# Packed weights of batches 4 to 7 made for four batches at once, as 64-row tiles, and sorted by batch through DRAM

## The chip, the cores and the metric

The kernel runs on one core of a Trainium2 chip. The time is the device time of one execution in microseconds, as the median of repeated runs. The core's engines work side by side, each in the order of its own queue: TensorE (PE; its weight loads, PEld, are listed apart), VectorE (DVE), ScalarE (ACT), GpSimd (POOL) and SyncE (SP). POOL and SP here mostly start DMAs.

## What is computed

Three stages, in fp32. First an attention in two steps: 32 packed queries `p` per head attend to `k` and `v`, and the result serves `q` as keys and as values.

```python
batch, n_heads, seq, head_dim = (8, 8, 576, 64); n_pack = 32
p_packed = sm_attn(p, k, v)             # softmax(p k^T / 8) v: [8, 8, 32, 64]
out = sm_attn(q, p_packed, p_packed)    # [8, 8, 576, 64]
x = out.transpose(0, 2, 1, 3).reshape(4608, 512)
h = x @ w_in                            # 512 -> 2048
x = (h / (1 + exp(-1.702 * h))) @ w_out # 2048 -> 512
h = max(x @ w1, x @ w2, x @ w3)         # 512 -> 768
return h @ w_out2                       # 768 -> 512
```

## The kernel before

Products are made from split operands: each fp32 value is held as a high and a low part in a reduced format, and `mm3` (line 98) issues three matmuls, low x high, high x low and high x high, into one PSUM bank.

Since the attention's second step ends with a product by `p_packed`, the kernel never forms `x`. It multiplies `p_packed` into `w_in` first. The result, `pw`, has 8 x 32 = 256 rows for a batch instead of 512, and the first feed-forward layer is a product of the softmax weights `at` with `pw`. Heads come in two groups g of four; a chunk c (0 to 3) of `w_in` is 128 rows, two heads; n (0 to 3) is a quarter of 512 columns of the 2048.

The first feed-forward part (FF1) runs as 256 units. Unit n takes one batch, one half of 288 tokens (hf) and one chunk fc of 128 columns: `h_unit` is 6 matmuls, two groups by `mm3`, from `at` and `pw`; tanh on ScalarE, a product on VectorE; `g_unit` splits the result, `out_unit` is 12 matmuls into four accumulating banks `acc`, two units later. Batches 0 and 1 are units 0 to 63 in alternating pieces; from batch 2 on a batch takes 32 units, so batch 4 starts at unit 128, and its quarter n is first used by unit 128 + 4n.

`pw` of batches 0 and 1 is made by `pw1_unit`. For batches 2 to 7 two batches share a matmul: `sps[pr, g]` holds `p_packed` of the batches 2 pr and 2 pr + 1 with zeros where head and batch don't belong together, so that `pw_unit(pr, c, n)` (line 383) takes 128 rows of `w_in` and gives 128 rows of result, two heads by two batches by 32. There are 16 calls for each of the three pairs. Its bank is a `pa` tile; `evac` (line 127) casts it to the high part on ScalarE and subtracts on VectorE, once for each half of the partitions, straight into the two batches' `pw` tiles. `load_wi` (line 378) fetches the split `w_in` chunk from DRAM (`wsc`) on POOL's queue, into a tile of tag `x`, of which there are four; the FF1 output `x2` uses the same tag.

The attention of a batch and group is a `Group` with steps: `load_pk`, `split_pk`, `load_v`, `s1` (scores, into two `pa` banks), `sm1`, `t1` and `t1r` (transposes), `load_q`, `pv`, `pt` (line 296: transposes the result and puts its split into `sps`, and an unsplit copy into `ptf` for the second step), `s2`, `sm2`, `sm3`, `tr2`. `s1`, `pv` and `s2` write 64 columns each, in two tiles of the array. The pool `ps_a` has two banks, which s1, t1, t1r, pv, pt, s2 and the `pw` units share.

`main` (line 804) writes the order by hand. Every step is put in a list with a due time, `add(t, fn, ...)`, and the list is sorted; a step's instructions are issued in that order, and where a tile isn't free, another ready step may come first. `tn[n]` is the due time of unit n, 2.55 apart from unit 11 on, a planned time and no measured one. `attention(t, b, g, stretch, dq)` puts the steps of a group from t on, and delays `load_q`, `s2` and what follows by dq. For the pairs 2 and 3 (batches 4 to 7) the four groups start 20 apart from `tn[64]` and `tn[128]`, and the 16 `pw_unit` calls lie within the last 32 units ahead of the pair's first use (`R_`, line 39). After the last attention step (`last_at`, line 897) the conversion of the second layer's weights starts (`Piece`), 8.5 apart.

Of the kernel before, what the change touches and what calls it, by code (L numbers as in the profile page):

```python
# [8 lines left out]
F32 = mybir.dt.float32  # L9
F32R = mybir.dt.float32r  # L10
# [6 lines left out]
B, H, S, D, NP = 8, 8, 576, 64, 32  # L17
DM, DFF, DFF2 = 512, 2048, 768
NT = B * S
P = 128  # L20
TB = 512
# [7 lines left out]
KD = DM // P  # L29
NQ = DFF // TB  # L30
# [7 lines left out]
Q_ = [12, 9, 9, 8]  # L38
R_ = [32, 23, 17, 5]
# [4 lines left out]
def tile_packed_attention_moe(  # L44
# [13 lines left out]
    nc = tc.nc  # L58
# [5 lines left out]
    def stage_pool(name, bufs, side):  # L64
        return tc.alloc_tile_pool(name=name, bufs=bufs, side=side, reuse_waits="tile")
# [3 lines left out]
    spp = stage_pool("spp", 1, "right")  # L69
    ap_ = stage_pool("ap", 1, "right")  # L70
# [5 lines left out]
    dram = ctx.enter_context(tc.tile_pool(name="dram", bufs=1, space=bass.MemoryType.DRAM))  # L76

    def f(t):
        return t.bitcast(F32)
# [5 lines left out]
    def w_tile(name, dt=F32R):  # L85
        return wp.tile([P, 2, 2, TB], dt, tag="w", name=name)

    def u_tile(name, dt=F32):
        return up.tile([P, S], dt, tag="u", name=name)

    def x_tile(name, dt=F32):
        return up.tile([P, 4 * HALF], dt, tag="x", bufs=4, name=name)

    def pa_tile(name):
        return ps_a.tile([P, TB], F32, tag="pa", name=name)
# [21 lines left out]
    wsc = dram.tile([2, NQ, 2, P, 2, TB], F32R, name="wsc")  # L117

    wsa = dram.tile([9, P, 2, 2, 3, P], F32R, name="wsa")
    wss = dram.tile([9, P, 2, 2, 4, P], F32R, name="wss")  # L120


# [4 lines left out]
    def evac(o, hi, lo):  # L127
        nc.scalar.copy(hi, o)  # L128
        nc.vector.tensor_tensor(out=lo, in0=o, in1=f(hi), op=ALU.subtract)  # L129
# [69 lines left out]

    at = {}  # L200
    sps = {}
    ptt = {}

    class Group:
# [27 lines left out]

        def load_q(self):
            self.q = self.load_t(q, "q")


        def s1(self, hf):
# [58 lines left out]
        def pt(self):  # L296
            o = pa_tile(f"ptp_{self.n}")
            self.mm = nc.tensor.transpose(o[:, :P], self.pn, ident)
            o3 = o[:, :P].rearrange("p (c n) -> p c n", c=2)
            self.ptf = ap_.tile([P, 2, D], F32, tag="ptf", bufs=2, name=f"ptf_{self.n}")  # L300
            if self.b < 2:
                t = u_tile(f"pt_{self.n}", F32R)
                nc.gpsimd.memset(f(t).rearrange("p (x n) -> p x n", x=2)[:, :, D:D + P], 0.0)
                to = ptt[self.b, self.g] = [t[:, HALF * x:HALF * x + 2 * P] for x in range(2)]
            else:
                key = self.b // 2, self.g
                if key not in sps:
                    sps[key] = [
                        spp.tile([P, 2 * P], F32R, tag=f"sp{self.g}{x}", name=f"sp{x}_{key[0]}_{key[1]}")
                        for x in range(2)  # L310
                    ]
                to = sps[key]
            hi, lo = (
                t[:, D:D + P].rearrange("p (c n) -> p c n", c=2) if self.swap
                else t.rearrange("p (c n) -> p c n", c=4)[:, 0:4:3] for t in to
            )
            nc.scalar.copy(self.ptf, o3)
            evac(o3, hi, lo)
# [56 lines left out]
    wi = {}  # L375
    pw = {}
# [6 lines left out]
    def pw_unit(pr, c, n):  # L383
# [8 lines left out]
        for x in range(2):  # L392
            r = slice(D * x, D * x + D)
            t = pw[2 * pr + (x ^ c & 1), n][:, g]
            evac(o[r], t[r, 0], t[r, 1])


    def pw1_unit(b, g, n):
        if g == 0:
            pw[b, n] = w_tile(f"pw_{b}_{n}")  # L400
        o = pa_tile(f"pw_{b}_{g}_{n}")
        for c in range(2):
            t = ptt[b, g]
            w = wi[0, 2 * g + (c ^ b & 1), n]
            mm3(o, [x[:, c * P:c * P + P] for x in t], (w[:, 0], w[:, 1]), c == 0, c == 1)
        hi, lo = (pw[b, n][:, g, x] for x in range(2))
        if n < 1 and b == 0:
            nc.scalar.copy(hi, o)
            nc.tensor.matmul(o, nident, hi, start=False, stop=True, skip_group_check=True)
            nc.scalar.copy(lo, o)  # L410
        else:
            evac(o, hi, lo)
# [33 lines left out]
    start = {}  # L446
# [315 lines left out]
    def add(t, fn, *a):  # L762
        plan.append((t, len(plan), fn, a))
# [28 lines left out]
    tpt, tend = {}, [0.0]  # L792

    def attention(t, b, g, stretch, dq=0.0):
        ts = []
        for k, (dt, fn) in enumerate(Group(b, g).steps()):
            after = {9: 7, 13: 12, 12: 11, 11: 10, 10: 8, 8: 6, 6: 5, 5: 3, 3: 1, 4: 2, 1: 0}.get(k)
            tk = t + dt * stretch + (D_[k] if b == 0 else 0) + (dq if k in (7, 9, 11, 12, 13) else 0)
            ts.append(tk if after is None else max(tk, ts[after] + .05))
            add(ts[-1], fn)  # L800
        tpt[b, g] = ts[10] + .05
        tend[0] = max(tend[0], ts[-1])

    def main():
# [10 lines left out]
        tn = [0.0] * 300  # L815
        t = T0
# [31 lines left out]
        for n in range(NQ):  # L848
            def tc_(kk):
                base = 7 + 6.49 * kk if n == 0 else tn[start[0, n]] - 22 + 7 * (kk - 4 * n)  # L850
                return base + K_[kk]
            for g in range(2):
                t = tc_(kk)
# [8 lines left out]
                kk += 1  # L862


        for pr in range(1, B // 2):
            b0 = 64 * (pr - 1)
            for idx, (b, g) in enumerate([(0, 0), (1, 0), (0, 1), (1, 1)]):
                if pr == 1:
                    attention(tn[0] + 70 + 18 * idx, 2 * pr + b, g, 1.2, 0 * b)
                else:  # L870
                    attention(tn[b0] + 20 * idx + 2, 2 * pr + b, g, 1.2, 38 * b)
            for n in range(NQ):
                for c in range(KD):
                    qn = Q_[n] if pr == 1 else R_[n]
                    qs = 1 if pr == 1 else 3
                    nn = start[2 * pr, n] - max(1, int(qn) - int(c * qs))
                    tp = max(tpt[2 * pr, c // 2], tpt[2 * pr + 1, c // 2])
                    add(max(tn[nn - 7] + .3, tp - 8), load_wi, pr, c, n)
                    add(max(tn[nn] + .3, tp), pw_unit, pr, c, n)


        def open_late():
# [17 lines left out]
        for idx in range(18):  # L900
            pc = Piece(idx // 2, idx % 2)
            t = TP + idx * TP_[1] if idx < 14 else TB0 - 10 + (idx - 14) * 10.5
# [5 lines left out]
        for fc in range(NF2):  # L908
            t = max(TP + 14 * TP_[1] + TP_[2] * fc, tn[225])
# [11 lines left out]
        for n in range(9 * NBLK):  # L921
            j, r = divmod(n, 9)
# [24 lines left out]
    if True:  # L947
        main()
        for _, _, fn, a in sorted(plan, key=lambda s: s[:2]):
            fn(*a)  # L950
        late["f"].release()
        late["x"].release()
        spp.release()
# [53 lines left out]
```

## Time and profile before

| | |
|---|---|
| median of 3 runs | 1333.19 us (1333.18 to 1334.12) |
| the profiled execution | 1333.64 us, of which span 1331.5 us |
| TensorE busy | 1308.8 us, 98% of the span, 8614 matmuls |
| VectorE, ScalarE, GpSimd busy | 69%, 40%, 8% |
| FF1 and attention | to 783 us of the span |
| second feed-forward layer | 783 us to the end |

The rows below come from that one execution. A row of the timeline gives the start in us from the span's start, the duration in us, the engine, the line, the operation, output <- input tiles, shapes and how many like it follow one another. A matmul's listed duration overlaps the next one's: what it costs the engine is the step from its start to the next start. In brackets stand the idle time ahead of an instruction and what ended it.

### The profile page before, as it was taken

How to read it: one execution, taken by the hardware profiler on the slowest of the kernel's cores; microseconds unless marked ns; L12 is line 12 of the kernel's file. 1: busy time of each engine (PE TensorE's matmuls, PEld its weight loads, DVE VectorE, ACT ScalarE, POOL GpSimd, SP SyncE). 2: the span in 40 equal slices, each digit the busy share in tenths (PEclk: the TensorE clock that was granted, in tenths of full speed). 3: DMA queues.
4: the chain of work that ended last, by engine and by line, in shares of the span. 5: the costliest groups of instructions: out<-in, count | busy, mean ns of one | idle time of the engine just before them, and what ended most of it. 6: DMA issues, size and time to landing. Idle time of an engine off the chain costs nothing.

```text
span 1331.5 us, 22347 instructions
## 1 busy us (share of the span) xinstructions
PE 1308.8 (98%) x8614; PEld 1229.7 (92%) x8614; DVE 919.9 (69%) x1896; ACT 533.3 (40%) x1140; POOL 107.4 (8%) x218
## 2 busy tenths in 40 slices
PE   6899999999999999999999999999999999999998
PEld 5699898989999989999999999999899899999997
DVE  6899976874756565669999889736556467366461
ACT  3466544554445444446656442311311313123111
POOL 1200001100000000000000001001011011010000
PEclk9899999999999999999999999999999999999999
DMA  9697734643323331236655649847657476575451
GB/s 338 211 403 300 251 107 139 193 123 120 106 80 100 103 102 54 82 112 195 207 200 191 206 160 360 294 169 252 223 188 264 151 261 239 172 254 197 174 174 48
DMA packets 88875, 249.70 MB, mean 188 GB/s; under 512 B 10177, under 2 KB 39361, under 8 KB 81857
## 3 DMA queue, kind: packets, MB, share of 16 engines
q0 software_dynamic: 24640, 132.66, 29.2%
q1 hardware_dynamic: 64128, 115.62, 25.4%
q8 instruction: 68, 1.11, 0.3%
q14 instruction: 39, 0.31, 0.1%
HBM read 204.47 MB, written 43.78 MB: 186 GB/s over the span
## 4 chain that ended last, share of the span: by engine, by line
PE 92%; DVE 4%; DMA 2%; issue 1%; ACT 1%; SPq 0%; POOL 0%; ACTq 0%; DVEq 0%; POOLq 0%
PE acc L100 10%; PE p L101 10%; PE p L100 10%; PE p L102 10%; PE acc L102 10%; PE acc L101 9%; PE h L100 5%; PE h L102 5%; PE h L101 5%; PE accb L101 4%; PE accb L102 4%; PE accb L100 4%; PE pw L100 1%; PE pw L101 1%; PE pw L102 1%; PE pv L287 1%
## 5 line engine op out<-in xcount | busy, mean ns | idle before, releaser
L100 PE MATMUL acc<-g,wo 128*128 128x288 f32 x1024 | 303.6, 299 | 0.0
L102 PE MATMUL acc<-g,wo 128*128 128x288 f32 x1024 | 300.6, 294 | 0.0
L101 PE MATMUL acc<-g,wo 128*128 128x288 f32 x1024 | 299.6, 293 | 0.4 <-POOL g L468 0.3
L100 PEld LDWEIGHTS acc<-g,wo 128*128 128x128 f32 x1024 | 191.4, 188 | 10.5 <-issue 5.3
L101 PEld LDWEIGHTS acc<-g,wo 128*128 128x128 f32 x1024 | 192.2, 188 | 4.3 <-issue 1.0
L102 PEld LDWEIGHTS acc<-g,wo 128*128 128x128 f32 x1024 | 192.0, 188 | 1.6 <-issue 1.5
L460 ACT ACTIVATE t<-h 128x288 f32<-128x288 f32 x256 | 104.8, 410 | 181.7 <-PE h L102 179.8
L461 DVE SCALAR_TENSOR_TENSOR t<-t,h 128x288 f32<-128x288 f32 x256 | 114.7, 450 | 84.7 <-ACT t L460 83.3
L100 PE MATMUL h<-at,pw 128*128 128x288 f32 x512 | 155.2, 304 | 1.3 <-DVE t L461 1.1
L101 PE MATMUL h<-at,pw 128*128 128x288 f32 x512 | 151.7, 296 | 0.3 <-POOL at L125 0.3
L102 PE MATMUL h<-at,pw 128*128 128x288 f32 x512 | 151.3, 296 | 0.0
L466 ACT CAST g<-t 128x288 fp32r<-128x288 f32 x256 | 110.6, 433 | 93.6 <-DVE t L461 92.4
L468 DVE TENSOR_TENSOR g<-t,g 128x288 fp32r<-128x288 f32 x254 | 114.9, 453 | 34.7 <-ACT g L466 33.8
L681 DVE TENSOR_TENSOR u<-s,p 128x384 f32<-128x384 f32 x54 | 29.9, 553 | 119.1 <-PE p L102 119.1
L101 PE MATMUL p<-x_T,ws 128*128 128x384 f32 x324 | 108.2, 334 | 0.0
L100 PE MATMUL p<-x_T,ws 128*128 128x384 f32 x324 | 108.2, 334 | 0.0
L102 PE MATMUL p<-x_T,ws 128*128 128x384 f32 x324 | 108.1, 334 | 0.0
L100 PEld LDWEIGHTS h<-at,pw 128*128 128x128 f32 x512 | 96.3, 188 | 9.7 <-issue 5.6
L101 PEld LDWEIGHTS h<-at,pw 128*128 128x128 f32 x512 | 96.4, 188 | 1.7 <-POOL at L125 1.3
L102 PEld LDWEIGHTS h<-at,pw 128*128 128x128 f32 x512 | 96.4, 188 | 0.1
L711 ACT COPY s<-p 128x384 f32<-128x384 f32 x54 | 25.9, 479 | 161.8 <-PE p L102 161.7
L129 DVE TENSOR_TENSOR pw<-pw,pw 64x512 fp32r<-64x512 f32 (+1 forms) x110 | 74.9, 686 | 18.2 <-ACT pw L128 17.2
(175 smaller groups left out, 2637.1 us busy)
## 6 DMA issues: line engine op xcount, KB each, us to landing
ws<-wss POOLq DMA_DIRECT2D x54, 1024.0 KB, 7.6
wa<-wsa POOLq DMA_DIRECT2D x54, 768.0 KB, 4.6
wi<-wsc POOLq DMA_DIRECT2D x48, 512.0 KB, 3.9
k<-in_k SPq DMA_DIRECT2D x16, 576.0 KB, 4.2
q<-in_q SPq DMA_DIRECT2D x16, 576.0 KB, 3.9
x2d<-x SPq DMA_DIRECT2D x16, 576.0 KB, 4.0
wss<-ws SPq DMA_DIRECT2D x36, 256.0 KB, 4.0
xr<-x2d SPq DMA_DIRECT2D x24, 384.0 KB, 4.1
```

The source lines that it names most:

```text
L100: nc.tensor.matmul(o, al, bh, start=start, stop=False, skip_group_check=more)
L101: nc.tensor.matmul(o, ah, bl, start=False, stop=False, skip_group_check=more)
L102: nc.tensor.matmul(o, ah, bh, start=False, stop=stop, skip_group_check=more)
L129: nc.vector.tensor_tensor(out=lo, in0=o, in1=f(hi), op=ALU.subtract)
L287: self.mm = nc.tensor.matmul(o[x * D:x * D + D, :P], self.et[:, c * P + x * D:c * P + x * D + D], self.v[:, c, y * P:y * P + P], start=c = ...
L460: nc.scalar.activation(t, o, AF.Tanh, scale=0.5 * 1.702)
L461: nc.vector.scalar_tensor_tensor(out=t, in0=t, scalar=1.0, in1=o, op0=ALU.add, op1=ALU.mult)
L466: latest["act"] = nc.scalar.copy(g[:, 0], gt[n])
L468: latest["dve"] = eng.tensor_tensor(out=g[:, 1], in0=gt[n], in1=f(g[:, 0]), op=ALU.subtract)
L681: latest["dve"] = nc.vector.tensor_tensor(out=o, in0=a, in1=b, op=op)
L711: latest["act"] = nc.scalar.copy(self.s1, self.b1)
```

## The change

For the batches 4 to 7 `p_packed` is no longer put into `sps`. `pt` copies it, unsplit, to a DRAM tile `ptd` (8 pieces), and `load_q` reads it back for `s2`. `split_q` reads it a second time and puts the split into `sq[g]`, whose columns are ordered by chunk, then by the four batches: 4 x 32 = 128 columns, each with one head's 64 rows in the upper or the lower half of the partitions. No zeros are kept. `pwq_unit(c, n)` then multiplies each half, 64 rows, by the same half of the `w_in` chunk: two heads, each three matmuls of 512 columns on 64 rows of the array, in turns, into two `pa` banks. Each bank holds one head for four batches. Both are evacuated whole into tiles of tag `x` and stored to a DRAM tile `pwd` on SP's queue; `load_pw(b, n)` reads the batch's rows back with four DMAs on POOL's queue.

There are 16 calls of `pwq_unit` for 32 of `pw_unit`. The order changes with it: the first halves of the attention of all four batches (to `pt`) start from `tn[64]` on, the groups of batches 4 and 5 15 apart, those of 6 and 7 between them; the second halves of 6 and 7 stay after `tn[128]`, by a larger dq. `split_q` is due from `tn[92]`, the 16 `pwq_unit` from `tn[95]`, 6.9 apart (the last between units 135 and 136), `load_pw` 6 units ahead of the first use for batch 4 and 14 for the others. `last_at` moves from 496.15 to 482.15 of planned time.

```diff
+    ptd = dram.tile([8, P, 2, D], F32, name="ptd")
+    pwd = dram.tile([NQ, KD, 2, P, 2, TB], F32R, name="pwd")
...
         def load_q(self):
             self.q = self.load_t(q, "q")
+            if self.b >= 4:
+                self.ptf = ap_.tile([P, 2, D], F32, tag="ptf", bufs=2, name=f"ptq_{self.n}")
+                nc.sync.dma_start(self.ptf, ptd[2 * (self.b - 4) + self.g])
...
+            elif self.b >= 4:
+                nc.scalar.copy(self.ptf, o3)
+                nc.sync.dma_start(ptd[2 * (self.b - 4) + self.g], self.ptf)
+                return
...
+    def split_q(b, g):
+        if g not in sq:
+            sq[g] = [spp.tile([P, 2 * P], F32R, tag=f"sp{g}{x}", name=f"sq{x}_{g}") for x in range(2)]
+        t = ap_.tile([P, 2, D], F32, tag="ptf", bufs=2, name=f"ptr_{b}_{g}")
+        nc.sync.dma_start(t, ptd[2 * (b - 4) + g])
+        k = (b & 1) * 2 + (b - 4) // 2
+        for x in range(2):
+            r = slice(D * x, D * x + D)
+            hi, lo = (y.rearrange("p (c m) -> p c m", c=2)[r, :, k * NP:k * NP + NP] for y in sq[g])
+            evac(t[r, :, x * NP:x * NP + NP], hi, lo)
+
+    def pwq_unit(c, n):
+        g = c // 2
+        cs = slice(c % 2 * P, c % 2 * P + P)
+        w = wi.pop((2, c, n))
+        o = [pa_tile(f"pwq_{c}_{n}_{x}") for x in range(2)]
+        for k, (y, z) in enumerate(((1, 0), (0, 1), (0, 0))):
+            for x in range(2):
+                r = slice(D * x, D * x + D)
+                nc.tensor.matmul(o[x], sq[g][y][r, cs], w[r, z], start=k == 0, stop=k == 2)
+        for x in range(2):
+            t = x_tile(f"pws_{c}_{n}_{x}", F32R)[:, :2 * TB].rearrange("p (a b) -> p a b", a=2)
+            evac(o[x], t[:, 0], t[:, 1])
+            nc.sync.dma_start(f(pwd[n, c, x]), f(t))
+
+    def load_pw(b, n):
+        pw[b, n] = w_tile(f"pw_{b}_{n}")
+        k = (b & 1) * 2 + (b - 4) // 2
+        for y in range(2):
+            for x in range(2):
+                r = y * D + x * NP
+                nc.gpsimd.dma_start(
+                    pw[b, n][r:r + NP],
+                    pwd[n, (y ^ b & 1)::2, x, k * NP:k * NP + NP].rearrange("g p a b -> p g a b"),
+                )
...
+        for idx, (b, g) in enumerate(order):
+            attention(tn[64] + 15 * idx - 10, 4 + b, g, 1.2, 30 + 10 * b)
+        for idx, (b, g) in enumerate(order):
+            attention(tn[64] - 3 + 15 * idx, 6 + b, g, 1.2, tn[128] - tn[64] + 20 + 8 * idx)
...
+        tq = [max(tn[92], *(tpt[b, g] for b in range(4, B))) + 3 * g for g in range(2)]
+        for b in range(4, B):
+            for g in range(2):
+                add(tq[g], split_q, b, g)
+        for n in range(NQ):
+            for c in range(KD):
+                t = max(tn[95] + 6.9 * (4 * n + c), tq[c // 2] + 2)
+                add(t - 12, load_wi, 2, c, n)
+                add(t, pwq_unit, c, n)
+            for b in range(4, B):
+                add(max(t + 3, tn[start[b, n] - 6 - (8 if b > 4 else 0)]), load_pw, b, n)
```

## Rows read from the trace of the kernel before

**Rows 1.** The page: busy us and share by engine; chain that ended last.

```profile
PE 1308.8 (98%) x8614; PEld 1229.7 (92%) x8614; DVE 919.9 (69%) x1896; ACT 533.3 (40%) x1140; POOL 107.4 (8%) x218
...
PE 92%; DVE 4%; DMA 2%; issue 1%; ACT 1%; SPq 0%; POOL 0%; ACTq 0%; DVEq 0%; POOLq 0%
```

**Rows 2.** Stage table: stretch, its us, engines' busy us, clock, DMA share, GB/s.

```profile
209.00:292.00 83.00, 82.14 (x588) 74.03 (x585) 63.22 (x136) 44.70 (x101) 8.99 (x19) 1.00 0.54 164
...
450.00:540.00 90.00, 89.85 (x692) 81.13 (x691) 51.36 (x121) 40.17 (x104) 3.16 (x8) 1.00 0.25 80
...
610.00:660.00 50.00, 48.82 (x350) 47.17 (x349) 49.56 (x119) 31.63 (x69) 1.58 (x3) 1.00 0.65 212
```

**Rows 3.** Timeline of TensorE: the first matmul of two neighbouring FF1 units.

```profile
402.38 0.29 PE L100 MATMUL h<-at,pw 128*128 128x288 f32 x1
...
404.75 0.29 PE L100 MATMUL h<-at,pw 128*128 128x288 f32 x1
```

**Rows 4.** Groups of instructions by shape: count, busy us, mean ns, idle ahead.

```profile
L129 DVE TENSOR_TENSOR pw<-pw,pw 64x512 fp32r<-64x512 f32 x96 | 65.7, 687 | 17.3 <-ACT pw L128 16.5
...
L380 POOL DMA_DIRECT2D wi<-wsc x48 | 25.5, 532 | 287.2 <-PE pw L102 240.7 <-DVE a L337 9.8 <-DVE ws L576 9.7
...
L100 PE MATMUL pw<-wi,sp 128*128 128x512 f32 x48 | 19.3, 403 | 1.0 <-DMA wi<-wsc 0.9
```

**Rows 5.** Timeline of TensorE: a `pw` unit's first matmul, and what follows the unit.

```profile
442.30 0.40 PE L100 MATMUL pw<-wi,sp 128*128 128x512 f32 x1
...
443.01 0.29 PE L100 MATMUL acc<-g,wo 128*128 128x288 f32 x1
```

**Rows 6.** Timeline of TensorE around `s1` (L242), read in narrow windows.

```profile
450.01 0.29 PE L102 MATMUL h<-at,pw 128*128 128x288 f32 x1
450.23 0.46 PE L242 MATMUL s<-k,pbd 128*64 128x288 f32 x2
...
450.23 0.14 PEld L242 LDWEIGHTS s<-k,pbd 128*64 128x64 f32 x2 [0.16 <-issue]
...
450.53 0.41 PE L242 MATMUL s<-k,pbd 128*64 128x288 f32 x2
...
450.77 0.41 PE L242 MATMUL s<-k,pbd 128*64 128x288 f32 x2
...
451.36 0.40 PE L100 MATMUL acc<-g,wo 128*128 128x288 f32 x1
451.59 0.30 PE L101 MATMUL acc<-g,wo 128*128 128x288 f32 x1
```

**Rows 7.** Timeline of TensorE: the largest hole after 610 us.

```profile
626.63 0.40 PE L100 MATMUL h<-at,pw 128*128 128x288 f32 x1 [0.88 <-DVE t L461]
```

**Rows 8.** Timeline of VectorE: the second subtract of the unit of rows 5.

```profile
445.15 0.69 DVE L129 TENSOR_TENSOR pw<-pw,pw 64x512 fp32r<-64x512 f32 x1 [0.28 <-ACT pw L128]
```

**Rows 9.** DMA issues from 209 to 782 us: count, KB each, us to landing.

```profile
x2d<-x SPq DMA_DIRECT2D x14, 576.0 KB, 4.0
...
wsa<-wa SPq DMA_DIRECT2D x32, 192.0 KB, 2.0
...
wraw<-in_w SPq DMA_DIRECT2D x36, 128.0 KB, 3.7
...
xr<-x2d SPq DMA_DIRECT2D x4, 384.0 KB, 6.8
...
v<-in_vr SPq DMA_DIRECT2D x7, 64.0 KB, 3.3
```

**Rows 10.** Timeline: an `s1` and the second exponential that reads it.

```profile
317.01 1.19 PE L242 MATMUL s<-k,pbd 128*64 128x288 f32 x8
...
319.88 0.49 ACT L259 ACTIVATE e<-s,st 128x288 f32<-128x288 f32 x1
```

**Rows 11.** Timeline of TensorE: an `s1` in two parts.

```profile
267.63 0.71 PE L242 MATMUL s<-k,pbd 128*64 128x288 f32 x4
268.27 0.40 PE L100 MATMUL acc<-g,wo 128*128 128x288 f32 x1
```

More of the change, by code (lines that the diff above doesn't have):

```diff
@@ L201, in tile_packed_attention_moe @@
     sps = {}
+    sq = {}
     ptt = {}
@@ L862, in main @@
                 kk += 1
[L865 to L879, printed above, removed]
+        order = [(0, 0), (1, 0), (0, 1), (1, 1)]
+        for idx, (b, g) in enumerate(order):
+            attention(tn[0] + 70 + 18 * idx, 2 + b, g, 1.2)
+        for idx, (b, g) in enumerate(order):
+            attention(tn[64] + 15 * idx - 10, 4 + b, g, 1.2, 30 + 10 * b)
+        for idx, (b, g) in enumerate(order):
+            attention(tn[64] - 3 + 15 * idx, 6 + b, g, 1.2, tn[128] - tn[64] + 20 + 8 * idx)
+        for n in range(NQ):
+            for c in range(KD):
+                nn = start[2, n] - max(1, int(Q_[n]) - c)
+                tp = max(tpt[2, c // 2], tpt[3, c // 2])
+                add(max(tn[nn - 7] + .3, tp - 8), load_wi, 1, c, n)
+                add(max(tn[nn] + .3, tp), pw_unit, 1, c, n)
+        tq = [max(tn[92], *(tpt[b, g] for b in range(4, B))) + 3 * g for g in range(2)]
+        for b in range(4, B):
+            for g in range(2):
+                add(tq[g], split_q, b, g)
+        for n in range(NQ):
+            for c in range(KD):
+                t = max(tn[95] + 6.9 * (4 * n + c), tq[c // 2] + 2)
[3 more added lines that the diff above has]
+                add(max(t + 3, tn[start[b, n] - 6 - (8 if b > 4 else 0)]), load_pw, b, n)
         def open_late():
```

## The prediction, made before the changed kernel was run

> **What bounds the kernel now.** I read the page's busy shares and its chain of waits first. TensorE is busy 98% of the span and carries 92% of the chain [rows 1], so the time is TensorE's instruction stream with almost no holes. A cut in VectorE, ScalarE or DMA work pays only where one of them made TensorE wait. The stage table comes next [rows 2]: from 450 to 540 us VectorE is busy 51 of 90 us and TensorE 89.85. Only from 610 to 660 us is VectorE full, 49.56 of 50, and there TensorE has 1.2 us of holes. Last, the timeline of one FF1 unit: a unit (6 h matmuls, 12 acc matmuls) repeats every 404.75 - 402.38 = 2.37 us [rows 3], 0.132 us a matmul. This step from start to start is what an instruction costs; the durations of 0.29 and 0.40 us overlap.
>
> **What is removed.** The packed weights of batches 4 to 7 take 32 of the 48 calls of `pw_unit` [rows 4]; each is three 512-column matmuls, 443.01 - 442.30 = 0.71 us [rows 5], a step of 0.235. 32 x 0.71 = 22.7 us of TensorE, all on the path. With them go 64 casts, 64 subtracts of 0.69 us [rows 4] and 16 of the `wi` loads.
>
> **What is added on TensorE.** 16 calls of `pwq_unit`, each three pairs of matmuls; each pair has the two heads on 64 rows of the array each, into two banks. No row of before shows 64-row tiles. The nearest are the 64-column tiles of `s1` [rows 6]: the two weight loads start together, so do the two matmuls, and the pairs start at 450.23, 450.53 and 450.77, 0.24 us apart. That is no proof of overlap: 0.12 us a matmul is about the 0.132 of a full 288-column one. Loads starting together are what two tiles working side by side would give, and I take a pair at 0.235, the step of one 512-column matmul; one after the other it is 0.47. Less than 0.235 I exclude: every tile still streams 512 columns.
> The same rows price entering and leaving a tile shape. In: 450.01 to 450.23 is 0.22 instead of 0.132 (+0.09). The first pair takes 0.30 instead of 0.24 with 64-column weights; I double the excess for 128 columns, +0.11. Out: the fourth pair (450.77 + 0.24 = 451.01) to 451.36 is 0.35 instead of 0.24 (+0.10); then 451.36 to 451.59 is 0.23 instead of 0.132 (+0.10). Together 0.40 us. A unit is 3 x 0.235 + 0.40 = 1.11 us, 16 are 17.7 us. Net: 22.7 - 17.7 = **-5.0 us**; without the switch -11.4, without overlap 16 x (6 x 0.235 + 0.40) = 29.0, that is +6.3.
> The trace, then, leaves the overlap open, and my reading rests on the loads that start together. The Trainium skill, "TensorE: Matmul & The Clock Gate", section "Measured speedup vs the span model", gives 3.07 times for four 32-row tiles; scaled from that, as an estimate, a pair would be 0.235 x 4 / 3.07 = 0.31 us and the net -1.4 us instead of -5.0.
>
> **Evacuations.** A unit of before takes two casts and two subtracts on half the partitions; a unit of after takes as many on all 128, for twice the work. So VectorE and ScalarE lose half of these: 32 x 0.69 = 22 us of VectorE over the whole, and none is left from 610 to 660 us, where six units lay (12 subtracts, 8 us). There TensorE waited 0.88 us for the VectorE step of an h unit [rows 7]. The weight conversion (`Piece`) of the second feed-forward layer starts 14 us of plan earlier (`last_at` 496 to 482) and spreads into the room. I take **-1.0 us** (0 to -1.2, the holes of the window; a loss I exclude, since VectorE only loses work).
>
> **The trip through DRAM.** `pwq_unit(3, 3)` is due between units 135 and 136; its result is first used by unit 140 (batch 4, fc 12). On TensorE lie between: 1.11 + 4 x 2.37 = 10.6 us. The chain: matmuls 1.1; evacuation about 2.5 (in before 445.15 + 0.69 - 443.01 = 2.8 [rows 5, 8], where the second cast waited for the first subtract); the SP store 4.0; about 0.5 for the POOL issue behind the other half's; the load 3.7 [rows 9]. Sum 11.8, so TensorE waits **+1.2 us**, once. With the fastest store of the rows (2.0) and 2.2 for the evacuation it is 9.5 and no wait; with 6.8 us for both transfers 18.2, a wait of 7.6. Behind TensorE's wait nothing else can run but two acc units. The other 15 units have 5 or more units of room. POOL's 64 issues of 0.53 us [rows 4] less 16 are 25 us on an engine that is 8% busy [rows 1]: hidden. SP waits for each subtract before it issues a store; what queues behind (later q, k and v loads, x2d stores) is due units later.
> `split_q` reads eight 64 KB pieces back through the two buffers of tag `ptf`, which `load_q` of (5, 0) and (4, 1) also hold until their `s2`. At 3.3 us a load [rows 9] and about 1 us of splitting, the first four end some 12 us after `s2` of (5, 0); on TensorE `pwq_unit(0, 0)` comes 126.0 - 112.8 = 13 us after it (due times, with 2.37 us a unit and the steps above). No margin to speak of: **+0.5 us** (0 to 2).
>
> **The denser first half of attention.** Eight groups run s1 to pt between units 62 and 88 where four were, beside ten `pw_unit` calls of batches 2 and 3. `s1` holds both banks of `ps_a`, 317.01 to 319.88 and a cast time later [rows 10], 2.9 to 3.4 us. In the due order three or four of the eight meet a bank that is not free. Before, such a meeting did not stop TensorE: `s1` was cut in two with acc matmuls between [rows 11], at the price of one more switch: 268.27 - 267.63 = 0.64 for two pairs, less 2 x 0.24, and the slow first matmul, 0.3 us in all. Three cuts: **+1.0 us** (0 to 7.7, below). VectorE has room: 63 of 83 us were busy there [rows 2], and four more first halves are some 7 us.
>
> **Sum.** -5.0 - 1.0 + 1.2 + 0.5 + 1.0 = -3.3 us. The profiled execution took 1333.64 us (span 1331.5 and 2.1 us around it), which gives 1330.3; it lies 0.45 us above the median of 1333.19, so for the median **1329.9 us**. Two of the terms are waits that fall on single points, so the forecast's own range, all at their mild ends or most at the hard ones, is 1326.5 to 1334.
>
> **Rivals.**
> *Weights not loaded ahead.* Tiles overlap, but a pair's weights wait for the pair before. Each of the 32 later pairs then pays the 0.10 us of a 128-column load seen after the switch [rows 6]: +3.2, 1333.1 us. For it: no row shows 64-row tiles. Against it: in `s1` the later pairs follow at 0.24, with no load time between.
> By the skill's scaled pair of 0.31 us the time would be 1329.9 + 48 x 0.075 = 1333.5, the same outcome.
> *The change doesn't do what it says:* the heads run one after the other. +11.3, 1341.2 us, slower. For it: 0.12 us a matmul in [rows 6] is what a serial pair would also show. Against it: the loads start together.
> *Slower by the banks.* In units 63 to 82 TensorE waits instead of running other units. The waits, from the 2.9 and 3.4 us hold and the 2.8 us evacuation of a `pw_unit`: `pw` after `s1` of (4,0) 0.8, s1(6,0) behind a `pw` 2.2, s1(5,0) 0.6, pv(6,0) 1.6, s1(7,0) 2.2, s1(5,1) 0.3: 7.7 us instead of 1.0, 1336.6 us. It decides once about six of the 7.7 us stand as holes. Against it: [rows 11] and 82.14 of 83 us busy there [rows 2].
> *Slower by the store and reload.* 7.6 us at unit 140 instead of 1.2: 1336.3 us. For it: the 6.8 us loads in the same stretch [rows 9]; against it: DMA is idle most of 373 to 450 us by the other rows' 3.7 to 4.0.
> *No price for the switch* with 64-row tiles: -6.4, 1323.5 us.
>
> The Trainium skill, "TensorEngine Tiling (Array Packing)", section "Restrictions and Gotchas", has a rule against the change: row tiles must write different banks, which raises the pressure on PSUM. Here that is the third rival, at 1336.6 us. From unit 108 on no other user of the two banks is due beside `pwq_unit`, which no run here shows yet.
>
> **How the numbers follow.** Forecast 0.57, weights not ahead 0.14, serial 0.12, banks 0.08, reload 0.05, no switch price 0.04. 0.2% (2.7 us, what a measurement of this kernel can tell from no change) puts the lines at 1330.5 and 1335.9. Of the forecast's 0.57, 0.46 lies below 1330.5 and 0.11 between. Faster 0.46 + 0.04 = 0.50; same 0.11 + 0.14 = 0.25; slower 0.12 + 0.08 + 0.05 = 0.25. The range 1326.5 to 1337 holds the forecast, the second rival and both bank and reload cases, 0.84, and leaves out serial and no switch price, 0.16.
>
> **What would show it.** The two matmuls of a `pwq` pair start within 0.02 us and the pairs 0.24 us apart (serial: each 0.24); a unit takes 1.1 us of TensorE. VectorE falls by some 20 us, and the hole near 625 us is gone. At unit 140 TensorE waits about 1 us for a load of `pw`; s1 appears cut in two three more times between 200 and 300 us. Wrong if pairs step by over 0.3 us, if TensorE's holes between units 62 and 95 sum to over 3 us, or if `pwq` units are themselves cut in two, since then their halves can't overlap.

## The result, and the profile after

The changed kernel takes 1344.57 us (median of 5 runs, 1341.5 to 1345.54) against 1334.12 us for the kernel before (1333.18 to 1334.76): a ratio of 1.0076, interval 1.0065 to 1.0088. It is 0.8% slower, where 1329.9 us and "faster" were forecast. The profiled execution took 1345.24 us, its span 1343.4.

The page: busy us by engine, and the chain that ended last (compare [rows 1]).

```profile
PE 1311.5 (98%) x8614; PEld 1224.5 (91%) x8614; DVE 898.5 (67%) x1872; ACT 520.2 (39%) x1116; POOL 133.7 (10%) x266
...
PE 85%; DVE 7%; DMA 4%; ACT 2%; issue 2%; SPq 0%; POOL 0%; DVEq 0%; ACTq 0%
```

VectorE lost 21.4 us of work, as forecast. But the chain, which was 92% TensorE, is now 85%, and VectorE and DMA took the difference: TensorE waits. Where, the stage table tells (columns as in [rows 2]):

```profile
209.00:292.00 83.00, 82.25 (x585) 70.72 (x583) 60.34 (x138) 45.44 (x106) 9.73 (x22) 1.00 0.59 184
450.00:540.00 90.00, 89.46 (x655) 83.75 (x655) 48.54 (x102) 37.65 (x87) 19.22 (x36) 1.00 0.85 211
610.00:660.00 50.00, 45.48 (x328) 44.67 (x327) 42.47 (x107) 25.54 (x57) 1.34 (x3) 0.97 0.63 198
```

The first two stretches are nearly as busy as before (82.14 and 89.85 us). From 610 to 660 us TensorE lost 3.3 us against [rows 2], and VectorE, which was full there, is now idle 7.5 of 50 us. Of TensorE's waits after 600 us, this is the whole list (engine, line, what was waited for: us, times, longest):

```profile
PE h L100 <- DVE t L507: 7.2, 2, 3.9
PE acc L101 <- DVE g L514: 0.7, 2, 0.4
PE acc L100 <- DVE x L540: 0.4, 2, 0.2
```

That is 8.3 us, against 1.1 us in the kernel before, nearly all in two stops (timeline of TensorE, in brackets the idle time ahead of the instruction):

```profile
619.71 0.40 PE L100 MATMUL h<-at,pw 128*128 128x288 f32 x1 [3.91 <-DVE t L507]
...
714.25 0.61 PE L100 MATMUL h<-at,pw 128*128 128x288 f32 x1 [3.25 <-DVE t L507]
```

Behind both stands VectorE, which waits for a DMA (timeline of VectorE):

```profile
613.50 0.46 DVE L514 TENSOR_TENSOR g<-t,g 128x288 fp32r<-128x288 f32 x1 [0.16 <-ACT g L512]
618.59 0.69 DVE L574 SCALAR_TENSOR_TENSOR wa<-c,wraw 128x512 fp32r<-128x512 f32 x1 [4.64 <-DMA wsa<-wa]
619.20 0.45 DVE L507 SCALAR_TENSOR_TENSOR t<-t,h 128x288 f32<-128x288 f32 x1
...
713.07 0.43 DVE L565 TENSOR_SCALAR c_o<-wraw_o 128x512 int32<-128x512 int32 x1 [3.66 <-DMA wraw_o<-in_w_out]
```

VectorE runs in order. At 613.96 us it reaches a step of the weight conversion that needs a store (`wsa`, started at 612.01 us) to have landed, and waits 4.64 us; the `t` step of an FF1 unit is queued behind it (619.20) and TensorE's next h unit behind that (619.71). And this is what POOL had started shortly ahead of both stops, batch 7's reloads of packed weights, four transfers each (timeline of POOL):

```profile
609.22 2.12 POOL L439 DMA_DIRECT2D pw<-pwd  x4 [7.34 <-PE h L102]
...
702.82 2.10 POOL L439 DMA_DIRECT2D pw<-pwd  x4 [17.32 <-PE h L102]
```

The other two of batch 7's bursts, at 599.73 and 683.38 us, have no stop over 0.4 us behind them.

The DMA issues from 606 to 618 us say what that does to the transfers beside them (count, KB each, median us to landing):

```profile
pw<-pwd POOLq DMA_DIRECT2D x4, 256.0 KB, 6.5
wss<-ws SPq DMA_DIRECT2D x2, 256.0 KB, 3.8
wsa<-wa SPq DMA_DIRECT2D x1, 192.0 KB, 6.5
```

The `wsa` store took 6.5 us, where the same store took 2.0 us in [rows 9]. The Trainium skill, "DMA: Bandwidth & Descriptors", section "Issuing engines are not separate DMA queues", says that transfers started by different engines run on the same 16 DMA engines and interleave. The trace agrees in that the two were under way together: SP's store from 612.0 to 618.5 us, POOL's four loads started from 609.2 us on and landed from 613.7 to 618.2 us.

The stops cost a second time. The clock after them (window, us, busy us of the five engines, then the granted clock, DMA share, GB/s):

```profile
616.00:620.00 4.00, 0.29 (x2) 0.30 (x3) 1.41 (x3) 0.32 (x1) 0.00 (x0) 1.00 0.28 60
620.00:624.00 4.00, 4.00 (x22) 3.99 (x21) 2.82 (x10) 1.81 (x5) 0.00 (x0) 0.63 0.73 250
624.00:628.00 4.00, 4.00 (x31) 4.00 (x30) 3.75 (x9) 2.62 (x6) 0.00 (x0) 0.94 0.29 112
...
706.00:710.00 4.00, 4.00 (x32) 4.00 (x32) 3.41 (x10) 2.29 (x5) 0.00 (x0) 1.00 1.15 307
710.00:714.00 4.00, 0.99 (x8) 0.77 (x6) 0.93 (x3) 0.47 (x1) 0.00 (x0) 0.90 1.09 325
714.00:718.00 4.00, 3.75 (x15) 3.75 (x16) 4.00 (x10) 2.53 (x7) 0.00 (x0) 0.50 0.20 77
718.00:722.00 4.00, 4.00 (x25) 4.00 (x25) 3.79 (x9) 2.33 (x5) 0.00 (x0) 0.75 0.42 131
```

TensorE stood still, and behind each stop it ran for a while at the lower clock, 0.50 (1.2 of 2.4 GHz): 15 matmuls from 714 to 718 us, where there were 32 from 706 to 710 us. Summed over the five windows from 620 us on that are below 1.00, 4 us times what is missing, that is 1.5 + 0.2 + 0.4 + 2.0 + 1.0 = 5.1 us. Counted by units it comes out alike: from FF1 unit 180 to unit 228 the changed kernel falls 13.1 us behind the one without the reload (e1 below), 8.1 us of it are waits, and 5.0 are left.

**The account.** The sum of the prediction gave 1330.3 us for the profiled execution; it took 1345.24, 14.9 us more. Waits after 600 us: 8.3, where 0.1 was left in the sum (1.1 less the 1.0 that was booked as gain): +8.2. Half clock behind the two stops: +5.1. From 40 to 52 us the granted clock was 0.72 instead of 0.86: 12 x 0.14 = +1.7, which is this execution's and not the change's: FF1 unit 4 starts 1.8 us later than in the kernel before, and in e1 and e2 below, whose programs are the same up to 200 us, 0.2 us later and 0.2 us earlier. The waits between 372 and 512 us (1.1 and 0.5 us) came to what was booked for the trip through DRAM and `split_q` (1.7). That makes 15.0. That it closes to 0.1 us is in part luck: the waits that were measured there are others than the ones that were booked.

### The profile page after: what moved, and what is told of

It is laid out like the page before. It is cut to its first block, busy times and chain, and to the rows that moved or that the text cites. A ratio compares the mean times of both kernels' runs of the same rounds, so it can differ in the third digit from the quotient of the medians.

```text
span 1343.4 us, 22585 instructions
## 1 busy us (share of the span) xinstructions
PE 1311.5 (98%) x8614; PEld 1224.5 (91%) x8614; DVE 898.5 (67%) x1872; ACT 520.2 (39%) x1116; POOL 133.7 (10%) x266
## 3 DMA queue, kind: packets, MB, share of 16 engines
q8 instruction: 68, 1.11, 0.4%
## 4 chain that ended last, share of the span: by engine, by line
PE 85%; DVE 7%; DMA 4%; ACT 2%; issue 2%; SPq 0%; POOL 0%; DVEq 0%; ACTq 0%
PE p L101 10%; PE p L102 10%; PE p L100 10%; PE acc L100 8%; PE acc L101 8%; PE acc L102 8%; PE h L100 4%; PE h L102 4%; PE h L101 4%; PE accb L102 4%; PE accb L101 4%; PE accb L100 4%; PE pv L293 1%; DMA wsa<-wa 1%; PE s L335 1%
## 5 line engine op out<-in xcount | busy, mean ns | idle before, releaser
L102 PE MATMUL accb<-wo,g 128*128 128x512 f32 x216 | 84.1, 390 | 0.0
```

What stands on the lines that cost most here:

```text
L102: nc.tensor.matmul(o, ah, bh, start=False, stop=stop, skip_group_check=more)
```

## Experiments

The theory from these rows (T1): the reloads of batch 7 crowd the loads and stores of the weight pieces. The first rival (T2): the pieces, which start 14 us earlier, do it alone.

**e1: no reload for batch 7.**

```diff
+        if b == 7:
+            nc.gpsimd.memset(f(pw[b, n]), 0.0)
+            return
```

> The changed kernel with batch 7's four reloads of packed weights left out (the tiles are filled with zeros by POOL, so batch 7's first feed-forward layer has wrong weights; all TensorE, VectorE and ScalarE instructions stay). Theory T1 (the reload bursts of batch 7 crowd the second layer's weight pieces): the holes of 4.1 and 3.4 us and the half clock behind them (about 4.7 us) go; 1344.6 - 7.5 - 4.7 = 1332 to 1334 us. Rival T2 (the pieces' earlier start alone makes the holes): both holes stay, 1343 to 1345 us.

1331.71 us, ratio 0.9981 (0.9972 to 0.9991). T1 holds: 13 us are gone with 4 MB of transfers; beside them only the four fills on POOL are new. T2 falls: the pieces start as early as in the changed kernel and the stops are gone. After 600 us one wait of 0.2 us is left (TensorE's waits):

```profile
PE acc L100 <- DVE x L543: 0.2, 1, 0.2
```

This is also what the rest of the change is worth: -2.5 us by the ratio, -2.3 by the medians.

**e2: pieces at their old due times.** `last_at = max(...) + 14.0`.

> The changed kernel with the weight pieces of the second feed-forward layer due 14 us later, where they lay before the change; the reloads are as in the changed kernel. T1: the reloads still meet pieces, perhaps other ones, so at least one hole of 3 us or more with half clock behind it stays, 1338 to 1345 us. T2: the holes go, 1332 to 1334 us.

1354.08 us, ratio 1.0147 (1.0122 to 1.0171). The later start doesn't help: stops remain (2.1 us of an h unit's wait for VectorE at 629 us), and now the pieces are also done too late, so that the second layer begins with a wait of 6.7 us for VectorE.

**e5: the reloads in four parts on SP.**

```diff
+            for q in range(4):
+                add(tn[(183, 191, 211, 221)[n] + 2 * q], load_pwq, 7, n, q, nc.sync)
```

> The changed kernel with each of batch 7's four reloads cut into its four transfers, started two units (about 5 us) apart on SP's queue instead of all at once on POOL's. The bytes are the same. T1: no burst, the holes go or fall below 1 us each, 1332 to 1336 us. T2: unchanged, 1343 to 1345 us. If it is the total of bytes and not the burst: smaller holes on more places, 1337 to 1343 us.

1334.85 us, ratio 1.0011 (1.0001 to 1.0020). 9.7 us of the 13 are back with the same bytes. The rest of its waits after 600 us is 3.6 us; the longest, 1.7 us, has VectorE busy and not waiting.

**e6: reloads to 128 rows.** The four batches' rows alternate in DRAM, so a reload is one transfer of 1 MB to 128 partitions or two of 512 KB to 64.

> The changed kernel with the rows of the four batches interleaved in DRAM, so that a reload is one transfer to 128 partitions (even batches) or two to 64 (odd ones) instead of four to 32; same bytes. If the narrow shape makes the burst (T4): 4 KB pieces at about 174 ns instead of 360, the burst half as long, holes 0 to 2 us each, 1332 to 1338 us. If the bytes alone do it (T1 without T4): holes unchanged, 1342 to 1345 us.

1352.02 us, ratio 1.0128 (1.0111 to 1.0145): worse. The wider shape doesn't shorten the burst. Its 512 KB loads after 600 us took 7.2 us to landing, the 256 KB loads of the changed kernel 6.3; TensorE waited 7.8 us for VectorE's `t` step instead of 7.2. The rows also lie apart in DRAM now, which this run doesn't separate from the shape. TensorE waited 4.1 us more at 475 us; that place is taken up below.

**e9, e10, e11: burst, queue or place.** e9 starts the four parts on SP at one due time instead of two units apart. e10 and e11 leave them on POOL and make each wait for an FF1 unit, by a copy of four elements from that unit's g tile into the rows that the load then overwrites:

```diff
+            nc.gpsimd.tensor_copy(out=pw[b, n][r:r + NP, 0, 0, :4], in_=gt[u][r:r + NP, 1, :4])
```

> The spread kernel with the four transfers of a reload started back to back again, still on SP's queue. T1 (the burst is what hurts, whichever queue starts it): holes of 2 to 4 us come back, 1338 to 1346 us. Rival (POOL's queue was the cause, not the burst): as the spread kernel, 1333 to 1336 us.

1336.23 us, ratio 1.0021 (1.0010 to 1.0031). It doesn't separate anything: SP's instruction order put other transfers between the parts again (starts at 609.9, 612.2, 618.1 and 620.7 us, in e5 609.1, 611.3, 617.3 and 619.8).

> The changed kernel with batch 7's reloads held to their due units on POOL's own queue: each of the four transfers of a reload first lets POOL copy four elements of the g tile of unit 210, 212, 214, 216 (then 218 and on) into its rows, so that transfers start 2 units, about 5 us, apart instead of four at once as soon as a buffer is free. Same bytes, same queue, same four-batch units. T1 (four transfers at once crowd the pieces): no hole over 2 us, 1332 to 1336 us. Rival (POOL's queue itself is slow, however the transfers are spread): holes as in the changed kernel, 1340 to 1345 us.

1338.96 us, ratio 1.0038 (1.0025 to 1.0050).

> As the paced kernel, but the four transfers of a reload start together again, at units 210, 218, 226 and 234. If four at once is what hurts: each burst leaves a hole of 2 to 4 us where it meets a piece, 1338 to 1346 us. If it was only the place of the first two bursts (600 and 609 us, at the first pieces): 1332 to 1336 us.

1337.97 us, ratio 1.0029 (1.0017 to 1.0040). On POOL's queue, held to units 210 to 240, four at once and four spread cost the same, so "four at once" is not the cause. e10 fits neither of its ranges; e11 lies at the edge of T1's, with 4.1 us of `h` waits, the longest 2.6. e10 has few waits up to 700 us, and then one of 3.5 us of TensorE for ScalarE, which waits for VectorE, which waits for a load (timeline of VectorE):

```profile
732.74 0.43 DVE L572 TENSOR_SCALAR c<-wraw 128x512 int32<-128x512 int32 x1 [3.71 <-DMA wraw<-in_w]
```

What the kernels with the reload share is that it costs: 3.1 us (e5), 4.5 (e9), 6.3 (e11), 7.2 (e10) and 12.9 (as changed) above the kernel without it. Bursts on POOL's queue cost 12.9 us where POOL took them, as soon as buffers were free, and 6.3 us at units 210 to 234, so the place counts. Whether SP's queue (e5, e9) is the better one by itself isn't shown, since there the place differs too.

**e4, e12: the same bursts in the kernel before.** Each adds four times four 256 KB transfers from DRAM to DRAM that nobody reads.

> The kernel before with nothing of the change, but with four extra bursts on POOL's queue, each of four 256 KB transfers from DRAM to DRAM that nobody reads, due at units 182, 186, 210 and 218, where the changed kernel's batch 7 reloads are due. T1 (bursts crowd the weight pieces): TensorE gets holes of 2 us or more and half clock behind them, 1338 to 1344 us. If the bursts only hurt together with the rest of the change: 1333 to 1335.5 us.

1335.78 us, ratio 1.0014 (1.0005 to 1.0023), and no test of T1: nothing held the bursts back, and POOL started them between 30 and 155 us. e12 copies stored pieces, so that each burst has to wait for them:

```diff
+                nc.gpsimd.dma_start(pwe[n, r]..., wss[k, r]...)    # k = 2 + n, four parts r
```

> The kernel before with four extra bursts on POOL's queue, each of four 256 KB transfers from DRAM to DRAM that nobody reads. They copy what pieces 4 to 11 stored, so none can start before these stores have landed, some 655 to 705 us, in the middle of the pieces (in the earlier run of this kind the bursts had nothing to wait for and started before 155 us). T1: holes of 2 us or more behind some of them and half clock after, 1337 to 1344 us. If bursts alone do nothing without the rest of the change: 1333 to 1335.5 us.

1334.15 us, ratio 0.9997 (0.9988 to 1.0006), with bursts at 659.09, 678.64, 694.13 and 708.81 us. In the kernel before, 4 MB beside the pieces cost nothing. T1 alone is therefore too little.

**e13: those bursts in the changed kernel, without reload.**

> The changed kernel without batch 7's reloads (its tiles filled with zeros, so batch 7's first layer has wrong weights), and with the same four DRAM to DRAM bursts at the weight pieces that did nothing to the kernel before. If a burst of 1 MB hurts this kernel because VectorE, with 21 us less to do, now stands at each piece's load instead of behind its own work: holes of 1 to 4 us come back, 1335 to 1342 us. If the bursts are harmless here too, and only the reload's own writes hurt: 1331 to 1333.5 us.

1336.84 us, ratio 1.0025 (1.0014 to 1.0036): 5.1 us above e1. The stretch from 645 to 720 us (columns as in [rows 2]) in the kernel before:

```profile
645.00:720.00 75.00, 74.92 (x555) 73.78 (x555) 74.30 (x185) 45.17 (x100) 0.00 (x0) 1.00 0.59 195
```

e12:

```profile
645.00:720.00 75.00, 74.93 (x555) 73.82 (x554) 74.30 (x185) 45.26 (x100) 8.07 (x16) 1.00 0.76 251
```

e1:

```profile
645.00:720.00 75.00, 75.00 (x570) 74.91 (x569) 74.33 (x185) 45.23 (x100) 3.63 (x2) 1.00 0.61 201
```

e13:

```profile
645.00:720.00 75.00, 71.70 (x533) 70.27 (x532) 69.84 (x174) 41.80 (x93) 11.81 (x18) 1.00 0.76 243
```

e12 and e13 have the same DMA share, 0.76, but only in e13 VectorE and TensorE lose time. VectorE's busy share doesn't tell why: before the bursts came it was 74.30 of 75 us in the one kernel and 74.33 in the other. The difference is how far VectorE stands behind its loads. Take one piece in each: the SP issue of its last two loads, and VectorE's first step on it. The kernel before:

```profile
698.34 0.95 SPq L546 DMA_DIRECT2D wraw<-in_w  x2
...
705.85 0.42 DVE L519 TENSOR_SCALAR c<-wraw 128x512 int32<-128x512 int32 x1
```

e1:

```profile
665.78 0.96 SPq L595 DMA_DIRECT2D wraw<-in_w  x2
...
670.30 0.42 DVE L568 TENSOR_SCALAR c<-wraw 128x512 int32<-128x512 int32 x1
```

e13:

```profile
665.61 1.78 SPq L596 DMA_DIRECT2D wraw<-in_w  x2
...
672.41 0.43 DVE L569 TENSOR_SCALAR c<-wraw 128x512 int32<-128x512 int32 x1 [2.23 <-DMA wraw<-in_w]
```

From the second load's start to the step it is 7.0 us in the kernel before (median of pieces 4 to 14 in the same way), 6.3 in e12, 4.0 in e1; the loads land after some 3.5 us. In e2, with the reload and with pieces due when they were in the kernel before, it is 3.8, so pieces at their old times don't have the margin of the kernel before either. With 3 us of margin, as in the median before, a load that is late by 2 is not noticed; with half a microsecond it stops VectorE, and TensorE behind it.

**e14, e15: is it VectorE's lighter load?** The kernel before without the 64 subtracts of batches 4 to 7 (their packed weights keep only the high halves, POOL fills the low ones with zeros), without and with the bursts of e12:

```diff
-            evac(o[r], t[r, 0], t[r, 1])
+            nc.scalar.copy(t[r, 0], o[r])
+            nc.gpsimd.memset(f(t[r, 1]), 0.0)      # for batches 4 to 7
```

> The kernel before with the 64 subtracts of the packed weights of batches 4 to 7 left out (POOL fills the low halves with zeros, so these weights keep only their high halves); no bursts, no four-batch units. VectorE has 44 us less to do, about 8 us of it between 610 and 660 us. Only the 1.1 us of holes after 610 us can go: 1332 to 1334 us.

1343.62 us, ratio 1.0070 (1.0053 to 1.0087).

> The same relieved kernel before, with the four DRAM to DRAM bursts at the weight pieces that did nothing to the full kernel before. If VectorE's backlog was what protected the full kernel: VectorE now waits for loads of pieces, TensorE gets holes of 1 to 3 us, 1335 to 1340 us. If the four-batch units or the earlier pieces of the changed kernel are what makes bursts harmful: as without bursts, 1332 to 1334 us.

1353.33 us, ratio 1.0147 (1.0128 to 1.0166). I had expected no harm from e14. Taking VectorE work away, with TensorE's work unchanged and 64 fills added on POOL, made the kernel before 9.8 us slower, and bursts that were free now cost 9.7 us more. VectorE's waits of e14 from 590 to 760 us, then one of them and the stop of TensorE behind it (timelines):

```profile
DVE c L523 <- DMA wraw<-in_w: 15.8, 12, 3.1
...
608.71 0.43 DVE L523 TENSOR_SCALAR c<-wraw 128x512 int32<-128x512 int32 x1 [2.63 <-DMA wraw<-in_w]
...
610.62 0.40 PE L101 MATMUL acc<-g,wo 128*128 128x288 f32 x1 [2.87 <-DVE g L472]
```

In the kernel before that wait is 1.3 us in all. The margin fell to 3.8 us (the same median): VectorE stands at each piece as its load is about to land, and the FF1 steps queue behind it. So a lighter VectorE is enough to bring the stops, with one reserve: four of e14's five stops over 1 us lie between 610 and 641 us, where POOL's fills run too (the last ends at 648 us), and no run takes the subtracts out of the kernel before without the fills. It doesn't say why e1, with a margin as small, waits only 2.1 us for these loads: the order in which the two programs lay VectorE's instructions differs, and part of e14's 10 us of waits after 600 us (2.2 us) is for ScalarE's cast of packed weights.

**e3: one head after the other.** To price the overlap, the six matmuls of a unit in the order of heads:

```diff
-        for k, (y, z) in enumerate(((1, 0), (0, 1), (0, 0))):
-            for x in range(2):
+        for x in range(2):
+            for k, (y, z) in enumerate(((1, 0), (0, 1), (0, 0))):
```

> The changed kernel with the six matmuls of a four-batch unit ordered head by head (three of head 0, then three of head 1) instead of in pairs; same work, same banks. If pairs run side by side (theory): five steps of 0.235 us instead of three, 16 x 0.47 = +7.5 us on TensorE, 1350 to 1353 us. If the two heads never overlapped: unchanged, 1343 to 1346 us.

1344.76 us, ratio 1.0085 (1.0071 to 1.0099): unchanged. That doesn't mean that the heads never overlapped. The changed kernel (timeline of TensorE):

```profile
372.66 0.29 PE L102 MATMUL h<-at,pw 128*128 128x288 f32 x1
372.88 0.97 PE L427 MATMUL pwq<-wi,sq 64*128 64x512 f32 x6
373.78 0.41 PE L100 MATMUL acc<-g,wo 128*128 128x288 f32 x1
374.02 0.29 PE L101 MATMUL acc<-g,wo 128*128 128x288 f32 x1
```

and e3:

```profile
371.28 0.97 PE L427 MATMUL pwq<-wi,sq 64*128 64x512 f32 x6
372.19 0.41 PE L100 MATMUL acc<-g,wo 128*128 128x288 f32 x1
```

Six matmuls of 512 columns in 0.90 us: one after the other they would take 6 x 0.235 = 1.41. In e3 the second matmul starts 10 ns after the first (3 ns in the changed kernel). The trace doesn't name the heads, but a second matmul on the same rows would come 0.235 us later, so it is head 1's, though two of head 0's are ahead of it in the program. The Trainium skill, "TensorEngine Tiling (Array Packing)", section "Key Properties", says that tiles work independently and load and multiply in parallel; the trace agrees, and more: the order of issue didn't matter.

**v1 to v5: mends that did not make it faster.** v1 is e5 with the four-batch units 2 us later and 6.5 us apart. It aims at two waits near 377 and 472 us that e1 still has (TensorE's waits, 372 to 512 us):

```profile
PE acc L101 <- DVE g L517: 1.3, 1, 1.3
PE acc L100 <- ACT x L541: 1.2, 1, 1.2
```

The first lies in the splitting of the reread tiles. In the second a unit's `pws` tiles and the output sums `x2` share four buffers, and ScalarE waits for a `pwd` store to land; it cost 0.5 us in the changed kernel, 1.2 in e1, 2.3 in e2 and 4.1 in e6.

> The spread kernel with the 16 four-batch units started 2 us later and 6.5 instead of 6.9 us apart, so that the store that held up an x2 tile at 472 us (0.7 to 4.1 us of TensorE in the runs so far) is due 3.6 us earlier and the evacuations of the first unit meet less of the attention's tail (1.3 us). If both holes go: 1334.85 - 2.0 = 1332.8 us, and 1332 to 1334.5 with one of them moved elsewhere. If the holes are not from where these stores lie: 1334.9 us.

1337.53 us, ratio 1.0029 (1.0018 to 1.0039): the first wait fell to 0.4, the second stayed (1.4). TensorE's waits at the pieces are 3.0 us in its profiled execution, 3.6 in e5's; the 1.9 us between these two executions lie ahead of FF1 unit 4, where the programs are the same. What made v1's median 2.7 us longer than e5's stays open.

> The changed kernel with the loads of the weight pieces due 12 instead of 8 us ahead of their use; reloads as in the changed kernel. If the holes come from loads that land too late: smaller holes, 1335 to 1341 us. If from buffers that come free late (stores that land late): unchanged, 1343 to 1346 us.

1344.60 us, ratio 1.0079 (1.0066 to 1.0093), unchanged.

> The spread kernel with the loads of the weight pieces due 12 instead of 8 us ahead. If the rest of its holes (1.9 and 0.7 us, VectorE waiting for loads of pieces) come from late loads: 1332 to 1334 us. If not: 1334 to 1336 us.

1337.88 us, ratio 1.0033 (1.0021 to 1.0044): the holes at the pieces did come from late loads. The margin, measured as above, is 5.9 us (4.7 in e5), and TensorE's waits from 590 to 780 us are down to

```profile
PE acc L100 <- DVE x L545: 0.2, 1, 0.2
PE acc L101 <- DVE g L519: 0.2, 1, 0.2
```

The last FF1 unit starts at 779.28 us, with the reload; in e1, without it, at 779.33, and in the kernel before at 781.02. What v3 wins there it loses again as the second layer starts (TensorE's waits from 782 us on, VectorE's from 780 to 830 us, where it waits for a store of a piece):

```profile
PE p L100 <- DVE u L732: 3.6, 1, 3.6
...
DVE m L732 <- DMA wss<-ws: 5.9, 1, 5.9
```

> The changed kernel with every VectorE and ScalarE step of a weight piece due 3.5 us later and its loads due when they were, so that VectorE meets a piece later after its load's issue. If the margin between load and conversion is what was lost: the holes behind late loads shrink, 1336 to 1342 us; the wait for a store to free a buffer (4.6 us of VectorE) may stay. If not: 1343 to 1347 us.

1356.06 us, ratio 1.0167 (1.0153 to 1.0181).

> The spread kernel with the pieces' steps due 3.5 us after where they were, loads as before. If the margin is what the spread kernel still lacks: its holes of 1.9 and 0.7 us go, 1331.5 to 1334 us, the first version below the kernel before. If not: 1334 to 1337 us.

1339.54 us, ratio 1.0047 (1.0033 to 1.0061). From 620 to 745 us TensorE is busy without a hole, and the margin is 6.4 us; but it waits 2.0 us ahead of 620 us, and 3.0 us as the second layer starts.

So with the reload spread, a longer lead (v3) or later steps (v5) gave the margin back, and the stops at the pieces went with it. With the reload in bursts they did not: in v4 the median from load to step is 3.6 us, and in v2 the waits for the `t` step stayed (7.5 us from 590 to 780 us, the longest 3.7). There are two `raw` buffers, so the load after next can't start before VectorE has done with a piece, and steps that come later move the loads along. Why the second layer then starts late in v3 and v5 was not followed up. No version with the reload came below the kernel before; e5 is nearest.

## Why the prediction was wrong

- *Four-batch units, -5.0 us:* right. From the last h matmul to the first acc matmul it is 373.78 - 372.66 = 1.12 us, less the step of 0.13 that is there anyway; the first acc matmul's step is 0.24 instead of 0.13. Together 1.10 us a unit, worked out were 1.11. All 16 units are alike, 1.08 to 1.10 us, but for one with the wait at 472 us. Serial heads, weights not ahead and a free switch are out.
- *Cuts of `s1`, +1.0 us:* the banks did not stop TensorE: from 209 to 292 us it is busy 82.25 us, before 82.14. `s1` is cut in two five times between 200 and 300 us, before twice, as expected. Counted by steps from 150 us on, the eleven `s1` take TensorE 16.5 us, before 15.5: +0.9, nearly as booked.
- *The trip through DRAM at unit 140, +1.2 us:* nothing waited there (0 of 0 to 7.6). The upper end was added up wrongly: with 6.8 us for both transfers the terms give 17.7 and a wait of 7.1, and that rival's time 1335.8.
- *`split_q`, +0.5 us:* the size was right to within its range, the place was not. Its cost is VectorE's and ScalarE's time (1.1 us at 378 us), not the load.
- *A wait that I did not list:* `pws` tiles in the buffers of `x2`, 0.5 us here and up to 4.1 in variants.
- *"POOL's 64 issues ... hidden" and "the other 15 units have 5 or more units of room":* the step that failed first. It asked whether the reloads are in time and whether POOL has time, not what their 4 MB do to the transfers beside them. POOL took them ahead of their due units, at 599.7 and 609.2 us, at the first pieces: e1 against the changed kernel, 12.9 us.
- *VectorE's relief, -1.0 us, "a loss I exclude":* the step that failed second and made the first one dear. [Rows 2] showed VectorE full from 610 to 660 us and I read a brake on TensorE. ("Only" there was a misreading: it was as full from 645 to 720 us, 74.30 of 75.) It was a brake by 1.1 us; it was also what kept 3 us, in the median, between a load's landing and its use. e12 against e13 shows that, e14 with its reserve, and v3, where the stops go as the margin comes back.
- *The clock:* no term. 5.1 us, a third of what was missed, are TensorE at half clock behind two stops.

Without the reload, -2.5 us was measured. My terms for that kernel are -5.0 - 1.0 + 0.5 + 1.0 = -4.5; the waits of 1.3 and 1.2 us from 372 to 512 us, less the 0.5 that I had booked, are the 2.0 between.

## What to carry to other kernels

Price a new transfer twice: by when it must be there, and by whose transfers it meets on the way; an issue queue that waits only for free buffers runs ahead of the plan (here POOL's, by 30 units) and meets whatever is there. Before counting relief of a full in-order engine as gain, measure how far its steps stand behind their loads: if the backlog is what hides the landing, taking it away turns a late load into a stop of whatever is queued behind, and earlier loads can give it back (v3). A stop of a few microseconds of TensorE costs more than itself, so the clock after it belongs into the sum.

## What the runs showed of the hardware that I had not expected

Two 64-row tiles ran side by side whatever the order of issue: in pairs 0.90 us a unit, head by head 0.91 us; to enter the shape and leave it cost 0.40 us a unit (1.10 less 3 x 0.235). The granted clock fell to 0.50 behind stops of 3.9 and 3.3 us, and stayed at 1.00 behind the 1.3 us stop of e13 (706 to 707 us; 704 to 712 us at 1.00). A store of 192 KB took 6.5 instead of 2.0 us beside 1 MB of loads from another queue. An engine can be busy 99% of a stretch and still lack margin: 74.30 of 75 us with 7.0 us from load to step (before), 74.33 with 4.0 (e1).
